# Splitting one zero fill by hand over the sixteen transfer engines

## The chip, the cores and the metric

The kernel runs on one core of a Trainium2 chip. A core has five instruction engines (TensorE, VectorE, ScalarE, GpSimd and SyncE; PE, DVE, ACT, POOL and SP in the profile) and sixteen transfer engines, which carry out the DMAs that SyncE, ScalarE and GpSimd issue. The metric is the time of one execution on the device in microseconds (us). Before the change it is 600.05 us, the median of three runs (599.26 to 600.44).

## The reference

The reference runs one decode step of a transformer block (one token, a window of 4096 cached keys and values, a gated feed-forward part, layer norms modulated by a condition vector) and then its gradients. It returns the output and the gradient of ten inputs:

```python
    _const = dict(B_x=B_x)
    def _f(*_d):
        return _fwd_reference(**{'A_x': _d[0], 'A_k_cache': _d[1], 'A_v_cache': _d[2], 'A_wq': _d[3], 'A_wo': _d[4], 'B_w_gate': _d[5], 'B_w_up': _d[6], 'B_w_down': _d[7], 'c': _d[8], 'w_mod': _d[9], **_const})
    _out, _vjp = jax.vjp(_f, A_x, A_k_cache, A_v_cache, A_wq, A_wo, B_w_gate, B_w_up, B_w_down, c, w_mod)
    _grads = _vjp(grad_out)
```

What matters here are two of these gradients: those of the key cache and of the value cache, each 4 x 65536 x 128 in bf16. The attention reads only the last 4096 rows of the 65536, so in both gradients 61440 of 65536 rows per head group are zero. Those zeros have to be written: 126 MB, about half of all the bytes that the kernel moves.

## The kernel before

The kernel is one long hand-ordered program (no scheduler moves instructions; each engine runs its own in the order in which they were written). Its stages are: loads and the layer norm, the query projection, the scores and the softmax, two large products for the attention's gradient (L637 and L692), the feed-forward part with its three weight gradients (from about L1000), and a last stage, in which VectorE and ScalarE build the gradients of the output projection (`dwo`, stored by L1135), of the modulation weights (`sec`, stored by L1130, and `s2`, L1182), of the query projection (`dwq_tile`, L1178) and of the window's keys and values (`dK` and `dV`, L1171), and store each as soon as it stands. The last stores of that stage are issued by SyncE (`tail = nc.sync`), the others by GpSimd (three small rows, L251, apart).

The zeros are written beside all this, as 120 fills of one megabyte each. A region is 128 rows (partitions of the view, not of SBUF) of 8 KB. An ordinary fill reads a zeroed tile of 128 partitions with 2 KB each in an 8-bit type and writes it as 32-bit zeros, eight rows for each of the sixteen transfer engines. The list `zleft` holds the fills in the order in which `zero(n)` takes them; the tables `Z_Q` to `Z_END` say how many are taken at each point of the program. The last stage takes four (`Z_END = (1, 2, 1, 0, 0)`): number 116 ahead of the `dwo` stores, 117 and 118 together after the sixth `dwo` store, and 119 after the eighth.

Six of the 120 fills are narrow (`NARROW`). Their first eight rows are left to a separate fill at the start, and the rest is written by fifteen transfer engines rather than sixteen. The code does this by resetting the cursor that says at which transfer engine GpSimd's next DMA begins (`inc_swdge_sem(..., mode="reset_dge_cursor")`), issuing a small DMA of five rows (L162, `NS = SKIP + 1` with `SKIP = 4`), which moves the cursor by five, and then one of 120 rows read from 60 partitions (L165). One engine is so left out. The last narrow fill is number 113, just ahead of the last stage.

GpSimd's DMAs share eight semaphores in turn: each waits, on GpSimd, until the eighth DMA before it has landed, which is when all sixteen transfer engines have done their part of it. Within one transfer engine the parts of GpSimd's DMAs run in the order of their issue.

Of the kernel before, what the change touches and what calls it, by code (L numbers as in the profile page):

```python
# [10 lines left out]
P = 128  # L11
FP32 = mybir.dt.float32
# [46 lines left out]
def kernel(  # L59
# [26 lines left out]
    nc = tc.nc  # L86
# [17 lines left out]
    def vt(shape, name, dt=FP32):  # L104
        return pool.tile(shape, dt, name=name)
# [4 lines left out]
    ZW = 4096  # L110
    zeros = vt([P, ZW // 2], "zeros", FP8)
# [12 lines left out]
    for og in (out_2, out_3):  # L124
        for g in range(G):
            region = og[0, g, 0:SKW, :].rearrange("r d -> (r d)").rearrange("(p x) -> p x", p=P)
# [6 lines left out]
    zleft = []  # L133
    while narrow or wide:
        if narrow and (len(zleft) in NARROW or not wide):
            zleft.append((narrow.pop(0), True))
        else:
            zleft.append((wide.pop(0), False))
    nlen = len(NARROW)
    ncount = list(range(1, nlen + 1))  # L140
    NS = SKIP + 1
# [5 lines left out]
    def dep(later, earlier):  # L147
        tc.add_manual_dep(later.ins, earlier.ins.name,
                          mybir.DependencyInfo(mybir.DependencyClass.Sync, mybir.DependencyReason.DATA),
                          reason="pace")  # L150

    def zero(n, after=None):
        for _ in range(n):
            if len(zleft) <= keep[0]:
                return
            region, narrow_ = zleft.pop(0)
            first = None
            if narrow_:
                nc.gpsimd.inc_swdge_sem([], [], mode="reset_dge_cursor")  # L160
                n = nlen - ncount.pop()
                first = nc.gpsimd.dma_start(  # L162
                    out=rest[0:NS, 0:nlen * 128].rearrange("p (t x) -> p t x", t=2)[:, :, n * 64:(n + 1) * 64],
                    in_=zeros[0:NS, 0:64].rearrange("p (t x) -> p t x", t=1).broadcast_to([NS, 2, 64]))
                ins = nc.gpsimd.dma_start(  # L165
                    out=region[8:P, :].bitcast(FP32).rearrange("(t p) x -> p t x", t=2),
                    in_=zeros[0:60, :].rearrange("p (t x) -> p t x", t=1).broadcast_to([60, 2, ZW // 2]))
            else:
                ins = nc.gpsimd.dma_start(out=region.bitcast(FP32), in_=zeros[:, :])  # L169
            if after is not None:  # L170
                dep(first or ins, after)
# [292 lines left out]
    for j in range(KD):  # L464
        if j in (1, 2, 3):
            kT_unit(8 + 2 * j)
            kT_unit(9 + 2 * j)
        if 0 < j <= NT:
            for g in range(G):
                wqT_unit(j - 1, g, "AVAA"[g])  # L470
        for h in range(HQ):
            mm = nc.tensor.matmul(q_ps[:, h:h + 1], lhsT=wq_t[j][:, h * P:(h + 1) * P],
                                  rhs=h1_bf[:, j:j + 1], start=(j == 0 and h == 0), stop=(j == KD - 1),
                                  skip_group_check=True)
        zero(Z_Q[j], mm)
# [8 lines left out]
    for ch in range(8):  # L484
        ps = new_ps("sc_ps")
        for g in range(G):
            mm = nc.tensor.matmul(ps[32 * g:32 * g + 32, 0:512], lhsT=q_col2[:, HG * g:HG * g + 32],
                                  rhs=k_T[:, g, ch * 512:(ch + 1) * 512], start=True, stop=True,
                                  tile_position=(0, 32 * g))
        nc.scalar.copy(out=P_bf[:, ch * 512:(ch + 1) * 512], in_=ps[:, :])  # L490
        nc.vector.reduce_max(out=mx8[:, ch:ch + 1], in_=ps[:, :], axis=AX.X)
        if ch % 2:
            wqT_unit(KD - 1, ch // 2, "AV"[ch // 2 % 2])
        zero(Z_KC[ch], mm)
# [26 lines left out]
    rsum = vt([P, 1], "rsum")  # L521
    last = nc.vector.reciprocal(out=rsum, in_=ssum)
    zero(Z_SM, last)
    rs_ps = new_ps("rs_ps")[:, 0:P]
    nc.tensor.matmul(rs_ps, lhsT=rsum[:, 0:1].broadcast_to([P, P]), rhs=ident_f[:, :], start=True, stop=True)
# [811 lines left out]
```

## Time and profile before

| | |
|---|---|
| median of three runs | 600.05 us (599.26 to 600.44) |
| the profiled execution | 599.91 us, of which the span from the first to the last instruction is 598.1 |
| busy, of the span | PE 68%, DVE 56%, ACT 44%, POOL 27% |
| DMA | 45026 packets, 246.63 MB, 412 GB/s over the span |
| written to HBM, read from it | 185.60 MB, 60.30 MB |
| GpSimd's DMAs | 94.7% of sixteen engines' span |
| SyncE's DMAs | 13.2% |
| zero fills | 114 ordinary ones of 1024 KB, median 15.7 us from issue to landing; 6 narrow ones of 960 KB, 13.1 us |

A row of stretches in the profile gives the stretch, its length, the busy time of PE, PEld (weight loads), DVE, ACT and POOL with the number of instructions in brackets, the granted clock of TensorE, and for DMA the busy share of the sixteen engines and the GB/s that they moved. A row of the timeline gives start, duration, engine, line, operation, what it writes and reads, how many such instructions, and in square brackets how long the engine sat idle before it and what ended that. A row of the chain gives start, duration and what the time went to; the chain is followed back from the last instruction.

### The profile page before, as it was taken

How to read it: one execution, taken by the hardware profiler on the slowest of the kernel's cores; microseconds unless marked ns; L12 is line 12 of the kernel's file. 1: busy time of each engine (PE TensorE's matmuls, PEld its weight loads, DVE VectorE, ACT ScalarE, POOL GpSimd, SP SyncE). 2: the span in 40 equal slices, each digit the busy share in tenths (PEclk: the TensorE clock that was granted, in tenths of full speed). 3: DMA queues.
4: the chain of work that ended last, by engine and by line, in shares of the span. 5: the costliest groups of instructions: out<-in, count | busy, mean ns of one | idle time of the engine just before them, and what ended most of it. 6: DMA issues, size and time to landing. Idle time of an engine off the chain costs nothing.

```text
span 598.1 us, 11044 instructions
## 1 busy us (share of the span) xinstructions
PE 406.6 (68%) x4586; PEld 275.3 (46%) x4612; DVE 335.3 (56%) x641; ACT 265.0 (44%) x409; POOL 159.1 (27%) x253
## 2 busy tenths in 40 slices
PE   3997688999999989999973426245345196775120
PEld 3995334334344546546652426235234175575120
DVE  3654499999511010160018585687787887768170
ACT  2489514567212014213135265565664845883110
POOL 3113123222222212222222243323424263122100
PEclk9999699999999999999995565565555576855555
DMA  8999999999999999999999999999999999999996
GB/s 347 419 418 421 414 423 417 428 424 425 426 419 425 424 428 422 424 422 423 424 396 415 419 409 417 412 359 416 405 403 414 419 422 411 421 424 425 426 424 283
DMA packets 45026, 246.63 MB, mean 412 GB/s; under 512 B 5085, under 2 KB 5085, under 8 KB 24544
## 3 DMA queue, kind: packets, MB, share of 16 engines
q0 software_dynamic: 37536, 217.60, 94.7%
q1 hardware_dynamic: 7392, 28.32, 13.2%
q8 instruction: 36, 0.59, 0.4%
q14 instruction: 14, 0.11, 0.0%
q10 hardware_dynamic: 48, 0.01, 0.0%
HBM read 60.30 MB, written 185.60 MB: 411 GB/s over the span
## 4 chain that ended last, share of the span: by engine, by line
DMA 37%; PE 32%; DVE 17%; issue 5%; ACT 4%; POOL 1%; DVEq 0%; ACTq 0%; POOLq 0%
DMA out_dram<-arena 15%; DMA arena<-in_B_w_gate_dram 13%; PE b_ps L692 10%; DMA out_dram<-zeros 9%; PE n_ps L637 6%; DVE arena L210 6%; DVE arena L206 5%; DVE arena L193 4%; PE t_ps L599 2%; PE tp_side L837 2%; PE tp_wq L454 2%; PE w_ps L395 2%; PE tp_k L435 1%; PE fg L954 1%; ACT arena L456 1%
## 5 line engine op out<-in xcount | busy, mean ns | idle before, releaser
L692 PE MATMUL b_ps<-arena 128*128 128x512 bf16 x493 | 113.4, 379 | 1.1 <-issue 0.2
L169 POOL DMA_DIRECT2D out_dram<-zeros x114 | 62.5, 550 | 176.9 <-DMA out_dram<-zeros 52.8
L193 DVE TENSOR_TENSOR arena<-arena 128x2048 bf16<-128x2048 bf16 x64 | 76.5, 1223 | 2.3 <-PE n_ps L637 0.3
L692 PEld LDWEIGHTS <-arena 128*128 128x128 bf16 x512 | 48.7, 98 | 55.9 <-issue 2.9
L210 DVE CUSTOM_DVE_ANT_0 arena<-arena,scr 128x1024 bf16<-128x1024 bf16 x56 | 66.2, 1220 | 9.6 <-ACT scr L992 9.6
L637 PE MATMUL n_ps<-arena 128*128 128x512 bf16 x249 | 65.1, 378 | 6.9 <-DVE arena L193 5.0
L838 ACT COPY arena<-tp_side 128x1024 bf16<-128x1024 bf16 x54 | 52.8, 1014 | 32.5 <-PE tp_side L837 32.5
L954 PE MATMUL fg<-h_bf,arena 128*128 128x1 bf16 x448 | 16.1, 166 | 55.0 <-DMA arena<-in_B_w_up_dram 31.4
L837 PE MATMUL tp_side<-ident_bf,arena 128*128 128x128 bf16 x432 | 48.9, 297 | 3.7 <-ACT arena L838 1.9
L837 PEld LDWEIGHTS <-arena 128*128 128x128 bf16 x432 | 42.3, 139 | 6.2 <-issue 6.0
L637 PEld LDWEIGHTS <-arena 128*128 128x128 bf16 x256 | 24.6, 97 | 41.6 <-issue 16.2
L954 PEld LDWEIGHTS <-arena 128*128 128x128 bf16 x448 | 14.1, 105 | 58.1 <-DMA arena<-in_B_w_up_dram 33.4
L1166 ACT ACTIVATE arena<-ps_kv 128x512 bf16<-128x512 f32 x48 | 26.1, 680 | 31.1 <-PE ps_kv L1162 30.8
L241 ACT ACTIVATE arena<-scr,h 128x1024 bf16<-128x1024 bf16 x35 | 38.5, 1143 | 2.7 <-DVE dh2acc L210 2.3
L202 DVE CAST arena<-b_ps 128x512 bf16<-128x512 f32 x6 | 4.2, 692 | 61.6 <-PE b_ps L692 61.6
L210 DVE CUSTOM_DVE_ANT_0 arena<-arena,b1k 128x1024 bf16<-128x1024 bf16 x24 | 28.4, 1222 | 17.9 <-PE fg L972 17.9
L1162 PE MATMUL ps_kv<-junk,arena 8*128 8x128 bf16 x256 | 26.5, 299 | 16.7 <-DVE arena L206 14.8
L869 POOL DMA_DIRECT2D out_dram<-arena x28 | 22.2, 798 | 51.5 <-ACT arena L241 35.4
L601 ACT CAST arena<-t_ps 128x512 bf16<-128x512 f32 x56 | 30.1, 589 | 12.1 <-PE t_ps L599 12.1
L1162 PEld LDWEIGHTS <-arena 8*128 8x128 bf16 x256 | 24.6, 138 | 18.4 <-issue 18.4
L456 ACT COPY arena<-tp_wq 128x1024 bf16<-128x1024 bf16 x23 | 21.7, 1041 | 8.1 <-PE tp_wq L454 8.1
L206 DVE TENSOR_SCALAR arena<-arena,cs_col 128x4096 bf16<-128x4096 bf16 (+1 forms) x16 | 16.1, 1019 | 12.5 <-DMA out_dram<-arena 12.4
(305 smaller groups left out, 639.2 us busy)
## 6 DMA issues: line engine op xcount, KB each, us to landing
out_dram<-zeros POOLq DMA_DIRECT2D x114, 1024.0 KB, 15.7
out_dram<-arena POOLq DMA_DIRECT2D x27, 1024.0 KB, 20.4
out_dram<-arena POOLq DMA_DIRECT2D x30, 512.0 KB, 11.6
out_dram<-arena SPq DMA_DIRECT2D x20, 512.0 KB, 10.1
arena<-in_A_wq_dram POOLq DMA_DIRECT2D x8, 1024.0 KB, 20.4
arena<-in_A_wo_dram POOLq DMA_DIRECT2D x8, 1024.0 KB, 12.3
arena<-in_w_mod_dram POOLq DMA_DIRECT2D x7, 1024.0 KB, 17.9
arena<-in_B_w_down_dram SPq DMA_DIRECT2D x14, 512.0 KB, 9.4
```

The source lines that it names most:

```text
L169: ins = nc.gpsimd.dma_start(out=region.bitcast(FP32), in_=zeros[:, :])
L193: return nc.vector.tensor_tensor(out=out, in0=a, in1=b, op=op)
L206: return nc.vector.tensor_scalar(out=out, in0=a, scalar1=s1, scalar2=None, op0=op0)
L210: return nc.vector.tensor_tensor_reduce(out=out, in0=w, in1=b, scale=1.0, scalar=0.0, op0=ALU.mult, op1=ALU.add, accum_out=acc)
L241: return nc.scalar.activation(out=out, in_=b, func=ACT.Copy, scale=col)
L601: nc.scalar.copy(out=o, in_=ps)
L637: mm = nc.tensor.matmul(nbank[k][:, :], lhsT=k_nat[:, g, t_ * DH:(t_ + 1) * DH], rhs=vp[:, t_ % 2, 4 * k:4 * k + 4, :].rearrange("p h d -> ...
L692: mm = nc.tensor.matmul(bbank[p][k][:, :], lhsT=a4[:, p, h, :], rhs=wo_t[u][:, a, k * 512:(k + 1) * 512], start=(i == 0 and a == 0), stop= ...
L837: nc.tensor.transpose(tp[:, i * P:(i + 1) * P], blk[:, i * P:(i + 1) * P], ident_bf[:, :])
L838: nc.scalar.copy(out=blk if dst is None else dst, in_=tp[:, :])
L954: nc.tensor.matmul(gu[:, col:col + 1], lhsT=ug_v[:, q % 2, j // 4, j % 4, k, f0:f0 + 255:2], rhs=h2_bf[:, j:j + 1], start=(j == 0 and i == ...
L1162: nc.tensor.matmul(ps[:, t4 * DH:(t4 + 1) * DH], lhsT=rows[32 * g:32 * g + HG, t_ * P:(t_ + 1) * P], rhs=hd[32 * g:32 * g + HG, :], start= ...
```

## The change

Fill number 117, the first of the two after the sixth `dwo` store, is marked, and `zero` writes it in three DMAs instead of one, after a reset of the cursor: 8 rows read from two partitions, 96 rows read from eight and 24 rows read from six. By the marks in `PARTS`, (transfer engines, rows for each), that is four rows each for engines 0 and 1, twelve each for 2 to 9 and four each for 10 to 15, where the one DMA had eight for each. The rows, their values and their bytes stay the same.

```diff
@@ -136,6 +136,8 @@
             zleft.append((narrow.pop(0), True))
         else:
             zleft.append((wide.pop(0), False))
+    zleft[117] = (zleft[117][0], None)
+    PARTS = ((2, 4), (8, 12), (6, 4))
     nlen = len(NARROW)
     ncount = list(range(1, nlen + 1))
     NS = SKIP + 1
@@ -165,6 +167,16 @@
                 ins = nc.gpsimd.dma_start(
                     out=region[8:P, :].bitcast(FP32).rearrange("(t p) x -> p t x", t=2),
                     in_=zeros[0:60, :].rearrange("p (t x) -> p t x", t=1).broadcast_to([60, 2, ZW // 2]))
+            elif narrow_ is None:
+                nc.gpsimd.inc_swdge_sem([], [], mode="reset_dge_cursor")
+                a = 0
+                for k, rows in PARTS:
+                    ins = nc.gpsimd.dma_start(
+                        out=region[a:a + k * rows, :].bitcast(FP32).rearrange("(p t) x -> p t x", p=k),
+                        in_=zeros[0:k, :].rearrange("p (t x) -> p t x", t=1).broadcast_to([k, rows, ZW // 2]))
+                    first = first or ins
+                    a += k * rows
+                assert a == P
             else:
                 ins = nc.gpsimd.dma_start(out=region.bitcast(FP32), in_=zeros[:, :])
             if after is not None:
```

## The prediction

> **What bounds the kernel now.** Read first: the page's slices and its chain; then busy time by stage of the last 40 us, the end of the chain in order of time, and GpSimd's issues around the changed fill.
>
> ```profile
> span 598.1 us, 11044 instructions
> ...
> DMA  8999999999999999999999999999999999999996
> GB/s 347 419 418 421 414 423 417 428 424 425 426 419 425 424 428 422 424 422 423 424 396 415 419 409 417 412 359 416 405 403 414 419 422 411 421 424 425 426 424 283
> ...
> DMA 37%; PE 32%; DVE 17%; issue 5%; ACT 4%; POOL 1%; DVEq 0%; ACTq 0%; POOLq 0%
> ```
>
> The transfer engines are busy in every slice but the first and the last. After 515 us nothing else matters: PE's share falls, DMA's stays above 1.00 of sixteen engines (packets overlap a little).
>
> ```profile
> 568.20:580.00 11.80, 3.57 (x32) 3.30 (x31) 10.56 (x15) 2.39 (x4) 0.00 (x0) 0.50 1.01 424
> 580.00:590.00 10.00, 0.00 (x0) 0.00 (x0) 0.00 (x0) 0.00 (x0) 0.00 (x0) 0.50 1.02 425
> 590.00:598.10 8.10, 0.00 (x0) 0.00 (x0) 0.00 (x0) 0.00 (x0) 0.00 (x0) 0.50 0.39 162
> ```
>
> From 580 us no engine computes; only transfers are left. Cut into microseconds, the last stretch shows engines dropping out one after another:
>
> ```profile
> 591.00:592.00 1.00, 0.00 (x0) 0.00 (x0) 0.00 (x0) 0.00 (x0) 0.00 (x0) 0.50 0.94 389
> 592.00:593.00 1.00, 0.00 (x0) 0.00 (x0) 0.00 (x0) 0.00 (x0) 0.00 (x0) 0.50 0.63 258
> 593.00:594.00 1.00, 0.00 (x0) 0.00 (x0) 0.00 (x0) 0.00 (x0) 0.00 (x0) 0.50 0.39 160
> 594.00:595.00 1.00, 0.00 (x0) 0.00 (x0) 0.00 (x0) 0.00 (x0) 0.00 (x0) 0.50 0.18 74
> 595.00:596.00 1.00, 0.00 (x0) 0.00 (x0) 0.00 (x0) 0.00 (x0) 0.00 (x0) 0.50 0.06 25
> ```
>
> Full rate is 425 GB/s, so one engine moves 26.6. At 25 GB/s a single engine is working: the last 1.6 us of transfers belong to one engine. The end of the kernel is therefore the finish of the slowest engine, and the question is only which one it is and whether the change gives it more rows or fewer.
>
> **Which engine is last.** The trace has every packet with start, duration, size and queue, but no engine. A packet starts 3 to 4 ns before its engine's previous one ends, so I strung the packets into sixteen chains, backwards from the end. They finish at 596.33, then 594.76, 594.55, 594.52, 594.39, 593.50, 593.40, 593.36, 593.31, 592.91, 592.18, 592.01, 591.85, 591.81, 591.67 and 591.51 us. Of 79 packets of 8 KB between 531 and 575 us that took 311 to 700 ns instead of 309, 76 lie on the chain of 596.33 (two of the other three come right behind a 16 KB instruction fetch). So the last engine is a slow engine, not an unlucky one.
>
> The last narrow fill (L162 and L165, issued at 478.37 and 478.97) tells which engine that is. By the code its first part takes five rows and moves the cursor by five, its second takes 120 rows, eight each, on the fifteen engines after that: the engine at place 4 after the cursor's reset gets none. The sixteen completions of L162 end with 486.72 and 487.20; those of L165 fifteen times follow 2.25 to 2.30 us later, and once 0.19 us later, at 487.39. So the left-out engine was the latest of all, by 0.48 us. In the next two full fills it needs 2.55 and 2.62 us between completions, the others 2.45: the same slowness, packet by packet, as on the chain that ends last. I take place 4 to be that chain. Between 494 and 528 us chains cross and I can't follow it without a break; the reading stands on the signature at both ends.
>
> **The change, part by part.** Program order is the same on PE, DVE, ACT and SP; only the numbers of GpSimd's DMA semaphores shift by two. On GpSimd one issue becomes a cursor reset and three issues, of 8, 96 and 24 rows from 2, 8 and 6 source partitions. It is the fill issued at 494.47:
>
> ```profile
> 485.85 7.36 POOL L1135 DMA_DIRECT2D out_dram<-arena  x5 [3.51 <-DMA out_dram<-arena]
> 493.73 0.75 POOL L1135 DMA_DIRECT2D out_dram<-arena  x1 [0.52 <-DVE arena L206]
> 494.47 0.56 POOL L169 DMA_DIRECT2D out_dram<-zeros  x1
> 496.62 0.55 POOL L169 DMA_DIRECT2D out_dram<-zeros  x1 [1.59 <-DMA out_dram<-zeros]
> 499.41 0.77 POOL L1135 DMA_DIRECT2D out_dram<-arena  x1 [2.24 <-DVE arena L206]
> 502.01 0.53 POOL L1130 DMA_DIRECT2D out_dram<-arena  x1 [1.83 <-DMA out_dram<-arena]
> ```
>
> *Rows.* Before: eight rows of 8 KB on each engine. A fill packet follows the next after 303.7 ns (eight of them and the completion: 2.45 us). Places 2 to 9 get four more, 4 x 0.3037 = +1.21 us each; the other eight get 1.21 us less. Total bytes are unchanged. Place 4 is in the heavy set: +1.21 us. It never idles from there to its end (its chain has no gap but the overlaps named), so nothing absorbs this. Its slowness on fills, 0.10 to 0.17 us for eight rows, adds 0.05 to 0.09 for four: +0.07.
>
> *Two more transfers.* Each leaves a completion packet on each engine: 2.45 less 8 x 0.3037 is 0.02 us. Two: +0.04. A rule speaks for far more: the Trainium skill, "DMA: Bandwidth & Descriptors", section "Anatomy of one DMA — SWDGE (gpsimd) path", fits a transfer at 2.0 us plus its bytes. Taken in full for two transfers that would be +4.0 us, an estimate from that page; back-to-back fills here show the fixed part hidden, and the sum uses 0.02 us.
>
> *GpSimd's issues.* The reset before L162 stands between issues at 477.63 (0.75 long) and 478.37: no time seen; between 0 and the 0.6 us of an issue. Two more issues of 0.6 fall into waits of 1.59, 2.24 and 1.83 us that GpSimd has anyway. Cost 0. If that cover were gone, 1.2 us would delay issues whose transfers reach the engines some 15 to 20 us later: still 0.
>
> *The window of eight.* Each GpSimd transfer waits for the eighth before it. Three parts take three places, so the issues after them wait for transfers two further on, about 2 x 2.5 = 5 us later each: L1135 of 499.41 goes to about 504.4, L1130 of 502.01 to 507, of 511.93 to about 515.5. Behind the waiting instruction stand only GpSimd's next stores; DVE, ACT and SP wait for landings, not issues. The first engine reaches the L1135 of 499.41 at 514 us and the L1130 of 502.01 at 516.6, with 1.2 us less if it is in the light set: 8 us of slack. From 522 us the issues wait for data again, and the window holds only whole transfers. Cost 0; upper bound 5 us if the queue ran dry, which the slack excludes.
>
> *The tail's own chain.* It ends so:
>
> ```profile
> 544.14 24.02 DMA out_dram<-arena
> 568.16 0.03 issue
> 568.18 5.05 DVE arena L206 x8
> 573.23 0.09 issue
> 573.32 1.13 DVEq L1332
> 574.45 4.31 DVE arena L206 x6
> ```
>
> The 24.02 us transfer lands when the slowest engine has done it, so it and the last stores' issues (last at 579.71) move by about +1.3 too. The fastest engine finishes GpSimd's work at 577 (576 if light) and has SyncE's stores from 569 to 571 on: it doesn't run dry, and the slowest is never short. No second cost.
>
> Sum: 1.21 + 0.07 + 0.04 = +1.32 us. The profiled execution (span 598.1, whole 599.91, that is 0.14 under the median of 600.05) would go to 601.2; the median to 601.4. 0.2% of it, 1.2 us, is about what a measurement of this kernel can tell from no change.
>
> **Rivals.**
>
> A. *Another engine ends last: faster.* If the chain of 596.33 is a light one, it drops 1.21 us to 595.12, and the end is whichever is later, that or the best heavy one: one of 594.76 at +1.21 is 595.97. Gain 0.36 to 1.21: 598.8 to 599.7. It decides if the last engine is outside 2 to 9. For it: the break in my chains at 494 to 528 us. Against: the left-out engine was late and slow, and the last chain has its signature. The skill's page "DMA: Bandwidth & Descriptors", section "Latency and other measured facts", says that engines 7 and 15 are usually the slower ones. Were 15 last here, it would be a light one and the case would be this rival's; the narrow fill's completions name place 4 instead.
>
> B. *The rows don't split as said.* If the 96-row part spreads over all sixteen engines (six rows each), place 4 gets between seven and nine rows: -0.3 to +0.3 us, 599.7 to 600.4. For it: no fill of this shape is in the trace. Against: the narrow fill, 120 rows from 60 partitions, did leave one engine out.
>
> C. *More than the rows: a lag that grows.* Instruction fetches, 16 KB packets in queue 8, take about 1.0 us on one engine and set its next completion back by about 1.4; one is at 497.46, one at 515.88. If the shifted issues bring one more onto the slow engine, it is +1.3 + 1.4: 602.8. Nothing says that they move.
>
> **How the numbers follow.** Forecast 0.70, A 0.13, B 0.08, C 0.09. The forecast's rows alone give 1.21 and the other terms only add, but runs of one kernel differ by 1.2 us (599.26 to 600.44), so 0.53 of its 0.70 is slower by over 0.2% and 0.17 within. With C, slower 0.62; with B, within 0.25; A, counted as faster, 0.13. The range takes in B and half of A below and the lower part of C above: 599.6 to 602.3.
>
> **What would show it.** After the change, the last microsecond of transfers is again one engine at 25 GB/s, ending near 597.6; the rate falls from 389 about 1 us earlier than before for the light engines; the transfer that ends the chain lands at about 569.5; three L174 issues start near 494.5, 496.6 and 499. Wrong, if transfers end before 596.3 or no engine works alone for a microsecond.

## The result and the profile after

The changed kernel takes 601.11 us (median of 19 runs, 599.45 to 602.57), the kernel before on the same chips 599.67 (598.44 to 600.87): a ratio of 1.0022 with a 95% interval of 1.0013 to 1.0032, or +1.3 us (+0.8 to +1.9). The profiled execution took 600.93 us with a span of 599.1.

The page of the changed kernel, the span and the transfer engines' two lines:

```profile
span 599.1 us, 11046 instructions
...
DMA  8999999999999999999999999999999999999996
GB/s 349 418 418 420 415 426 411 426 426 423 428 419 425 422 427 424 421 423 425 422 397 412 420 411 416 411 369 413 404 405 416 420 420 412 405 423 427 426 421 266
DMA packets 45250, 246.63 MB, mean 412 GB/s; under 512 B 5309, under 2 KB 5309, under 8 KB 24768
```

The shape is that of before: transfers fill every slice but the first and the last. The bytes are the same, but there are 224 packets more, all under 512 B; the experiments come back to them.

The last stretch of the changed kernel, by microseconds (columns as before):

```profile
590.00:591.00 1.00, 0.00 (x0) 0.00 (x0) 0.00 (x0) 0.00 (x0) 0.00 (x0) 0.50 0.94 389
591.00:592.00 1.00, 0.00 (x0) 0.00 (x0) 0.00 (x0) 0.00 (x0) 0.00 (x0) 0.50 0.92 385
592.00:593.00 1.00, 0.00 (x0) 0.00 (x0) 0.00 (x0) 0.00 (x0) 0.00 (x0) 0.50 0.64 266
593.00:594.00 1.00, 0.00 (x0) 0.00 (x0) 0.00 (x0) 0.00 (x0) 0.00 (x0) 0.50 0.46 188
594.00:595.00 1.00, 0.00 (x0) 0.00 (x0) 0.00 (x0) 0.00 (x0) 0.00 (x0) 0.50 0.39 160
595.00:596.00 1.00, 0.00 (x0) 0.00 (x0) 0.00 (x0) 0.00 (x0) 0.00 (x0) 0.50 0.19 78
596.00:597.00 1.00, 0.00 (x0) 0.00 (x0) 0.00 (x0) 0.00 (x0) 0.00 (x0) 0.50 0.06 25
597.00:598.00 1.00, 0.00 (x0) 0.00 (x0) 0.00 (x0) 0.00 (x0) 0.00 (x0) 0.50 0.02 8
```

The last whole microsecond again belongs to one engine at 25 GB/s, one microsecond later than before, and the last packet ends at 597.38 us instead of 596.33. The rate is at 389 GB/s one microsecond sooner: the tail is longer at both ends, as it must be when some engines have more to do and others less.

The end of the chain of waits of the changed kernel (start, duration, what):

```profile
545.20 24.02 DMA out_dram<-arena
569.23 0.03 issue
569.25 5.67 DVE arena L218 x8
574.92 0.60 DVEq L1344
575.51 4.31 DVE arena L218 x6
```

The same chain as before, 1.06 us later from its transfer on. And GpSimd's issues around the fill, in order of time:

```profile
493.71 0.75 POOL L1147 DMA_DIRECT2D out_dram<-arena  x1 [0.52 <-DVE arena L218]
494.45 0.62 POOL L174 DMA_DIRECT2D out_dram<-zeros  x1
496.59 0.62 POOL L174 DMA_DIRECT2D out_dram<-zeros  x1 [1.53 <-DMA out_dram<-zeros]
499.03 0.67 POOL L174 DMA_DIRECT2D out_dram<-zeros  x1 [1.82 <-DMA out_dram<-arena]
501.55 0.56 POOL L181 DMA_DIRECT2D out_dram<-zeros  x1 [1.85 <-DMA out_dram<-arena]
504.32 1.27 POOL L1147 DMA_DIRECT2D out_dram<-arena  x1 [2.21 <-DVE dcs L222]
506.87 0.53 POOL L1142 DMA_DIRECT2D out_dram<-arena  x1 [1.28 <-DMA out_dram<-arena]
```

No time is to be seen for the reset between 493.71 + 0.75 and 494.45. The three parts go out at 494.45, 496.59 and 499.03, the second and the third each waiting (1.53 and 1.82 us) for a transfer that the one fill would not have waited for, and the next two stores leave at 504.32 and 506.87.

The packets themselves, strung together by their starts, show the slow engine in the stretch of the two fills. One row of 8 KB per entry, start in us and duration in ns; the bar marks the next fill:

```
before  510.81:322 511.09:354 511.40:384 511.73:365 512.05:388 512.39:379 512.70:384 513.04:361
      | 513.40:336 513.68:374 514.01:384 514.35:369 514.65:388 514.99:361 515.31:349 515.62:359
after   510.56:326 510.84:367 511.16:365 511.48:369 511.80:369 512.11:384 512.45:374 512.78:360
        513.09:385 513.43:365 513.75:355 514.07:381
      | 514.48:322 514.75:356 515.06:384 515.39:380 515.73:355 516.03:366 516.34:361 516.66:374
```

Before the change other engines' rows take 322 ns (the first of a DMA) and 348 (each one after it) here, so one engine stands out with mostly 354 to 388. It had eight rows in the changed fill before and has twelve after. From the first row to the next fill's first row it took 2.59 us before and takes 3.92 after: +1.33 us.

Strings of packets can be exchanged where two engines' packets end within a nanosecond or two, and no slow packet marks the engine after 575 us. So that this engine is the one that ends last is a reading. An estimate from the durations agrees with it. At its first row above, before the change, the engine is the twelfth of sixteen to start the fill, 0.15 us ahead of the latest. From there to the end its slow packets take about 1.5 us more in all than the others' of their size (311 to 420 ns against 309, and 355 to 420 against 348), and the last engine ends 1.57 us behind the next.

### The profile page after: what moved, and what is told of

The parts are those of the page before. It is cut to its first block, busy times and chain, and to the rows that moved or that the text cites. A ratio compares the mean times of both kernels' runs of the same rounds, so it can differ in the third digit from the quotient of the medians.

```text
span 599.1 us, 11046 instructions
## 1 busy us (share of the span) xinstructions
PE 406.3 (68%) x4586; PEld 273.9 (46%) x4612; DVE 335.8 (56%) x641; ACT 264.9 (44%) x409; POOL 161.6 (27%) x255
## 4 chain that ended last, share of the span: by engine, by line
PE 45%; DMA 22%; DVE 19%; issue 5%; ACT 5%; POOL 0%; ACTq 0%; DVEq 0%; POOLq 0%; SPq 0%
PE b_ps L704 18%; DMA out_dram<-arena 14%; DVE arena L222 7%; PE n_ps L649 6%; DVE arena L218 5%; DMA arena<-in_B_w_down_dram 4%; DVE arena L205 4%; DMA arena<-in_B_w_gate_dram 3%; PE t_ps L611 2%; PE tp_side L849 2%; PE fold_ps L888 2%; PE tp_wq L466 2%; PE w_ps L407 2%; PE tp_k L447 1%; PE bc_ps L309 1%
```

## The experiments

Each of the kernels below is the changed kernel with the lines shown, and was timed against the kernel before on the same chip. A second measure comes from the packets of the profiled execution: the bytes that GpSimd's and SyncE's queues have still to move, at 508 us and at 528, compared with the kernel before and divided by the full rate. What grows between the two is what the sixteen engines lost, on average, while the changed fill and its neighbours were transferred; in the change itself it is 0.60 us, and after 528 us nothing more is lost.

**Equal rows in three parts.** The split without the redistribution.

```diff
-    PARTS = ((2, 4), (8, 12), (6, 4))
+    PARTS = ((2, 8), (8, 8), (6, 8))
```

> The same three parts after the same reset, but eight rows for every transfer engine: ((2, 8), (8, 8), (6, 8)). Theory 1, the rows decide (the engine at place 4 ends last, and its rows move the end): as before, plus 0.04 us for two more completion packets: ratio 1.000, last packet near 596.4 us, a single engine at the end for 1.6 us. Theory 2, the split itself costs (reset, two more issues, three of eight places in the window): as the changed kernel, ratio 1.0022 to 1.0024, last packet 597.4 or later. Theory 3, another heavy engine than place 4 ends last: as theory 1 here.

Measured: 600.69 us against 599.53, ratio 1.0019 (1.0008 to 1.0030). The split costs about as much as the change does although each engine has its eight rows: theory 1 alone doesn't hold here. The end in the trace is neither theory's: the last packets end at 596.67 and 596.52 us, in an execution of 600.13 us, 0.56 below this kernel's median.

**The heavy eight moved off place 4.**

```diff
-    PARTS = ((2, 4), (8, 12), (6, 4))
+    PARTS = ((5, 4), (8, 12), (3, 4))
```

> The same uneven pattern moved on by three places: four rows each for places 0 to 4, twelve for 5 to 12, four for 13 to 15: ((5, 4), (8, 12), (3, 4)). Place 4 is light now. Theory 1: place 4 ends 1.21 us earlier, at 595.12; of the others the latest, 594.76, ends at 595.97 if it became heavy: the last packet lies between 595.1 and 596.0, ratio 0.9980 to 0.9994. Theory 2, the split costs whatever the rows: ratio 1.0022 to 1.0024. Theory 3: the last engine is one of places 5 to 9, heavy in both: 1.0022; or one of 2 and 3, light here: as theory 1.

Measured: 600.85 us, 1.0017 (1.0005 to 1.0028). The slow engine has four rows here (509.73 to 510.64 us, then eight from 511.12), and the chain that holds 70 of its slow packets between 531 and 575 us ends eighth, at 594.16. Another ends at 596.68. So place 4 was relieved, and the time is still 1 us above before.

**24 rows for places 4 and 5.**

```diff
-    PARTS = ((2, 4), (8, 12), (6, 4))
+    PARTS = ((4, 4), (2, 24), (2, 4), (8, 7))
```

> Twenty-four rows each for places 4 and 5, four each for 0 to 3, 6 and 7, seven each for 8 to 15: ((4, 4), (2, 24), (2, 4), (8, 7)). Sixteen rows more on place 4. Theory 1: its end moves by 16 x 0.3037 = 4.86 us and the slowness of sixteen fill rows, 0.2 to 0.3: +5.1 us, last packet near 601.4, ratio 1.0085. Theory 2: as the changed kernel, ratio 1.002 to 1.003. Theory 3, place 4 is an engine that ends between 591.5 and 594.8: 4.86 us on top of that is 596.4 to 599.7, so +0 to +3.3 us, ratio 1.000 to 1.0055.

Measured: 605.23 us, 1.0088 (1.0071 to 1.0105), +5.7 us by the medians. The slow engine has 24 rows in one run from 510.27 to 517.8, and the chain with 72 of its slow packets ends last, at 600.72:

```profile
598.00:599.00 1.00, 0.00 (x0) 0.00 (x0) 0.00 (x0) 0.00 (x0) 0.00 (x0) 0.50 0.13 53
599.00:600.00 1.00, 0.00 (x0) 0.00 (x0) 0.00 (x0) 0.00 (x0) 0.00 (x0) 0.50 0.11 45
600.00:601.00 1.00, 0.00 (x0) 0.00 (x0) 0.00 (x0) 0.00 (x0) 0.00 (x0) 0.50 0.04 16
```

Two engines at 25 GB/s each until 599.88 us, and then one: rows do count where the slow engine gets them.

**Places 4 and 5 made light, in four parts.**

```diff
-    PARTS = ((2, 4), (8, 12), (6, 4))
+    PARTS = ((4, 10), (2, 2), (2, 10), (8, 8))
```

> Two rows each for places 4 and 5, ten each for 0 to 3, 6 and 7, eight for 8 to 15: ((4, 10), (2, 2), (2, 10), (8, 8)). Theory 1: place 4 ends 1.82 us earlier, at 594.51; the next, 594.76, keeps its eight rows and is then last: -1.57 us, ratio 0.9974, and a candidate that beats both kernels. Theory 2: ratio 1.002 to 1.003. Theory 3, the last engine is among those with ten rows: +0.6 us, 1.001; among those with eight: 1.000.

Measured: 601.55 us, 1.0031 (1.0018 to 1.0044). The slow engine has its two rows (510.10 and 510.40, the next fill from 510.93), and it doesn't help: what the four parts and the ten rows on six other engines cost is more than place 4 gives back. This run alone doesn't divide the two. Between 508 and 528 us these kernels lost 0.86 (equal), 0.64 (moved), 1.10 (24 rows) and 1.00 us (four parts).

What do the parts lose? Two lines of stretches for the changed kernel, then for the three equal parts:

```profile
508.00:512.00 4.00, 2.75 (x53) 2.27 (x53) 2.14 (x12) 4.00 (x7) 0.53 (x1) 1.00 1.11 393
512.00:516.00 4.00, 3.00 (x32) 0.90 (x31) 3.59 (x8) 3.08 (x7) 2.31 (x2) 1.00 1.09 395
```

```profile
508.00:512.00 4.00, 3.36 (x61) 2.40 (x49) 1.86 (x14) 4.00 (x8) 1.01 (x2) 1.00 1.09 377
512.00:516.00 4.00, 2.54 (x27) 0.85 (x27) 4.00 (x7) 1.98 (x5) 0.76 (x1) 1.00 1.10 382
```

and for the kernel before:

```profile
508.00:512.00 4.00, 3.22 (x58) 2.56 (x58) 1.69 (x11) 4.00 (x7) 0.60 (x2) 1.00 1.09 427
512.00:516.00 4.00, 2.69 (x32) 0.71 (x27) 3.91 (x8) 2.61 (x6) 1.00 (x2) 1.00 1.14 423
```

The busy share stays at or above 1.09 while 423 to 427 GB/s become 377 to 395: the engines don't run dry, their packets take longer. Between 506 and 519 us the kernel before has 7 packets that are long (8 KB over 400 ns or 4 KB over 240), the equal parts 43, up to 682 ns for 8 KB, and the change 32, up to 840. And there are new packets of 4 bytes. Both could go back to the shape of the parts: two, eight and six source partitions, hence as many engines, and the others idle. Four more kernels separate this.

**The reset, and one DMA from sixteen source partitions.**

```diff
-    PARTS = ((2, 4), (8, 12), (6, 4))
+    PARTS = ((16, 8),)
```

> The cursor reset and then one DMA of 128 rows, read from 16 source partitions, eight rows of each: every transfer engine gets eight rows, none stands idle. The first four runs left the split itself as the main cost (three parts with eight rows for every engine: 0.19% slower, with 508 to 516 us of the trace at 377 to 382 GB/s in place of 423 to 427). Theory I (parts that leave transfer engines without rows are what costs): 0, within 0.05% of before, 508 to 516 us at 420 GB/s or more. Theory N (each further DMA costs some 0.55 us): 0. Theory S (rows read again and again from a few source partitions cost): as much as the three equal parts, +1.1 us, about 380 GB/s. Theory R (the reset costs): +1.1 us.

Measured: 599.91 us against 599.85, 1.0005 (0.9989 to 1.0021); lost 0.12 us, 10 long packets. Neither the reset nor reading one partition eight times costs anything that shows.

**Three parts, each on all sixteen engines.**

```diff
-    PARTS = ((2, 4), (8, 12), (6, 4))
+    PARTS = ((16, 3), (16, 3), (16, 2))
```

> The reset and then three DMAs of 48, 48 and 32 rows, each on all sixteen engines (three, three and two rows each). Theory I: 0, no long packets between 508 and 516 us. Theory N: +1.1 us, as with the three equal parts. Theory S: between 0 and +1.1 us, since each partition is read two or three times in one DMA. Theory R: +1.1 us.

Measured: 600.14 us, 1.0007 (0.9994 to 1.0020); lost 0.10 us, 11 long packets. Two more transfers in themselves lose next to nothing, so by the packets theory N falls. The time alone would leave room for its 1.1 us (1.0018); the kernels with three parts and other sources below, at most 1.0014 and 1.0004, don't.

**Three parts, engines idle for one row only.**

```diff
-    PARTS = ((2, 4), (8, 12), (6, 4))
+    PARTS = ((16, 7), (2, 1), (14, 1))
```

> The reset and then three DMAs: seven rows for each of sixteen engines, one row for each of two, one for each of the other fourteen. All engines get eight rows, two of the three parts leave engines without rows, but for one row's time only: 16 packets without rows if there is one for each row that a used engine has, where the three equal parts had 256. Theory I: +0.1 us (16 of 256) if it is those packets, and a packet count of 45026 plus 16 plus 32. Theory N: +1.1 us. Theory S: +1.0 us (seven rows from one partition). Theory R: +1.1 us.

Measured: 599.76 us, 1.0010 (0.9996 to 1.0024); lost 0.22 us, and 45074 packets: exactly one packet of 4 bytes for each row that a used engine has, on each engine that has none.

**The source partitions sixteen apart.**

```diff
-    PARTS = ((2, 4), (8, 12), (6, 4))
+    PARTS = ((2, 8), (8, 8), (6, 8))
...
-                        in_=zeros[0:k, :].rearrange("p (t x) -> p t x", t=1).broadcast_to([k, rows, ZW // 2]))
+                        in_=zeros[0:16 * k:16, :].rearrange("p (t x) -> p t x", t=1).broadcast_to([k, rows, ZW // 2]))
```

> The three equal parts (eight rows for every engine, from 2, 8 and 6 source partitions), but the source partitions lie 16 apart instead of side by side. Theory I: +1.1 us as before, 377 to 382 GB/s from 508 to 516 us. Theory N: +1.1 us. Theory S in the form that neighbouring source partitions hinder one another: near 0, no packets of 8 KB longer than 400 ns. Theory S in the form that one partition is read too often: +1.1 us. Theory R: +1.1 us.

Measured: 599.77 us, 1.0000 (0.9986 to 1.0014); lost 0.28 us, 18 long packets, up to 558 ns. The 4-byte packets are all there, as in the equal parts, and partition 0 is still read by three engines; yet most of the loss is gone. That speaks against theory I, and in theory S for the form in which neighbouring partitions hinder one another, though that form expected no row over 400 ns.

**Equal parts, each with source partitions of its own.**

```diff
-    PARTS = ((2, 4), (8, 12), (6, 4))
+    PARTS = ((2, 8), (8, 8), (6, 8))
...
-                a = 0
+                a = o = 0
                 for k, rows in PARTS:
...
-                        in_=zeros[0:k, :].rearrange("p (t x) -> p t x", t=1).broadcast_to([k, rows, ZW // 2]))
+                        in_=zeros[o:o + k, :].rearrange("p (t x) -> p t x", t=1).broadcast_to([k, rows, ZW // 2]))
                     first = first or ins
                     a += k * rows
+                    o += k
```

> The three equal parts (eight rows for every engine) again, but each part reads source partitions of its own, the first 0 and 1, the second 2 to 9, the third 10 to 15, so that the sixteen engines read sixteen different partitions, where they read partition 0 three at a time before. The packets without rows stay: 45314 packets in all. Theory P (several engines reading the same few source partitions is what costs; the sources 16 apart had brought the loss from 0.85 to 0.33 us): 0, 508 to 516 us at 415 GB/s or more, no 8 KB packets over 500 ns. Theory I (the packets without rows, or the idle engines, cost): +0.6 to +1.1 us and about 380 GB/s as with the three equal parts.

Measured: 599.72 us against 599.50, 0.9991 (0.9978 to 1.0004), where the same parts with shared partitions gave 1.0008 to 1.0030 on another chip. The stretches, and the packets of the page (the profiled execution, 601.82 us, is the longest of the twelve):

```profile
508.00:512.00 4.00, 3.54 (x127) 3.25 (x125) 4.00 (x8) 4.00 (x6) 1.00 (x2) 0.78 1.05 406
512.00:516.00 4.00, 2.90 (x58) 2.52 (x58) 1.71 (x11) 4.00 (x7) 2.31 (x3) 1.00 1.17 422
```

```profile
DMA packets 45314, 246.63 MB, mean 411 GB/s; under 512 B 5373, under 2 KB 5373, under 8 KB 24832
```

The packet count of the equal parts is kept; 8 KB packets over 500 ns are gone, 15 long ones are left, and the loss is 0.23 us, of which the 4-byte packets are some 0.1 (256 of them, about 6 ns apart on their engine, over sixteen engines). The first stretch is below the 415 GB/s that theory P expected. Theory P has the place right and the reason too narrow: the partitions sixteen apart were shared between engines as before and lost no more than this. What the cheap kernels have in common is that the sixteen engines' reads don't all lie in partitions 0 to 7, as they do in the change; that crowding is the greater part of the split's cost. What it is about these eight partitions that makes it slow, no run shows.

**The change, with source partitions of its own.** The lines of the kernel just above, with the rows of the change:

```diff
-    PARTS = ((2, 8), (8, 8), (6, 8))
+    PARTS = ((2, 4), (8, 12), (6, 4))
```

> The change as it is (4, 12 and 4 rows), with source partitions of its own for each part. Theory P with the rows of the prediction (place 4 is the last engine and gets four more): +1.2 us, last packet 1.2 us later than that of the equal rows with own sources. Theory P alone (only the sources cost, the rows are absorbed): 0. Theory I: +1.3 us as measured for the change, 393 GB/s from 508 to 516 us.

Measured: 601.00 us against 599.50, 1.0023 (1.0010 to 1.0036); lost 0.24 us instead of 0.60. With the reading made cheap the rows alone cost what the change costs. The kernel just above differs from this one in its rows only and was timed on the same chip: 601.00 against 599.72 is 1.28 us by the medians (1.9 by the two ratios), where the prediction has 1.21 and 0.07 for the rows and the slowness. The chain with 78 slow packets ends last, at 597.02. The expectation's last packet can't be compared, since that of the equal rows comes from their longest execution (598.28).

**24 rows for places 6 and 7.** Own source partitions again.

```diff
-    PARTS = ((2, 8), (8, 8), (6, 8))
+    PARTS = ((6, 4), (2, 24), (8, 7))
```

> 24 rows for engines 6 and 7, four for 0 to 5, seven for 8 to 15, each part with source partitions of its own; the run with 24 rows for 4 and 5 took 5.70 us more than before. If place 4 is the slow engine that ends last (the prediction's reading): 6 and 7 end between 591.51 and 594.76 us before the change, 16 rows more are 4.86 us, so the end goes to between 596.4 and 599.6, +0.1 to +3.3 us, middle value +1.6. If any engine with 24 rows ends so late: +4.8 to +5.7 us.

Measured: 602.25 us, 1.0031 (1.0012 to 1.0050): +1.9 us by the ratio, +2.75 by the medians, within what place 4's reading gave and far from the 5.7 of the pair 4 and 5. That pair had shared sources, but the 1.10 us that its engines lost on average don't make up the difference. The end of this kernel:

```profile
596.00:597.00 1.00, 0.00 (x0) 0.00 (x0) 0.00 (x0) 0.00 (x0) 0.00 (x0) 0.50 0.13 53
597.00:598.00 1.00, 0.00 (x0) 0.00 (x0) 0.00 (x0) 0.00 (x0) 0.00 (x0) 0.50 0.08 33
598.00:599.00 1.00, 0.00 (x0) 0.00 (x0) 0.00 (x0) 0.00 (x0) 0.00 (x0) 0.50 0.07 29
```

Two engines to 597.35, then one to 599.15, neither of them the slow one: its four rows lie from 509.17 to 510.52 us, and the chain with 60 of its packets ends ninth, at 594.01.

**The reverse of the change.** Nine rows for each place but 4 and 5, one for these, own source partitions; meant to beat both kernels.

```diff
-    PARTS = ((2, 8), (8, 8), (6, 8))
+    PARTS = ((4, 9), (2, 1), (10, 9))
```

> The reverse of the change: nine rows for engines 0 to 3 and 6 to 15, one row for 4 and 5, in three parts with source partitions of their own. If place 4 is the engine that ends last and reading different partitions makes the split cheap: place 4 goes from 596.33 to 596.33 - 7 x 0.3037 + 0.25 = 594.45 us, and the next best from 594.76 to 594.76 + 0.30 + 0.25 = 595.31, so the last packet comes 1.0 us earlier and the time is 0.17% below that of before; the chain with the slow packets is no longer the last. If place 4 is not the last engine: +0.3 to +0.6 us, a row more on the last one and the parts' own packets.

Measured: 600.09 us against 600.04, 0.9997 (0.9983 to 1.0010); the last packet ends at 596.91. No gain, and the packets show that in this execution the slow engine was not relieved:

```
        510.80:326 511.08:455 511.50:388 511.83:402 512.18:398 512.52:379 512.86:365 513.18:355 513.49:372
      | 513.86:325 514.14:372 514.47:388 514.81:379 515.13:359 515.45:371 515.77:388 516.08:382
```

Nine rows, not one, and the other engines' packets show where the parts went. An engine with a row in the second part alone would get nine packets of 4 bytes ahead of that row. Instead the two single rows come right behind nine rows and a completion:

```
nine rows from 508.81, completion 511.51:52, one row 511.56:322, next fill from 511.94
nine rows from 509.10, completion 511.80:52, one row 511.85:322, next fill from 512.23
```

Two engines get no row: the next fill's first rows at 509.43 and 510.44 us come behind 23 packets of 4 bytes, as many as the three parts and the store before them leave on such an engine. That accounts for all 128 rows: fourteen engines with nine, two of these with one more, two with none. So the second part fell on two of the first part's four engines: the cursor stood two places on, not four. The third part then began at place 4, and nine rows are what place 4 should get. The runs with 24, four and two rows put the slow engine at place 4 too, and so does the last narrow fill of this very execution, among whose rows no slow packet shows.

Why nine rows from each of four partitions leave the cursor there, where four rows (the pair 4 and 5) and ten (the four parts) let the next part reach place 4, no run shows. So this kernel doesn't relieve the slow engine, and what a relief with own sources and no heavy pair elsewhere would gain is not measured.

## Why the prediction was right, point by point

**What ends the kernel.** Right: the slowest transfer engine, alone at 25 GB/s; predicted to end near 597.6, measured 597.38, which is 1.05 us later than before where 1.32 were forecast. The transfer that ends the chain was expected to land at about 569.5; it lands at 569.22.

**Which engine it is, and its rows.** Right for the change: the packets show twelve rows in place of eight on the slow engine. The terms for the rows, the slowness and the transfers, +1.32 us together, stand against +1.33 us from its first row to the next fill. Five more kernels agree in the count of its rows (four, 24, two, twelve with own sources, and four), and so does the reverse of the change (nine), with the cursor that its packets show. The two pairs with 24 rows, 5.7 us for one and 1.9 to 2.75 for the other, show that it matters which engine gets them. With own sources the rows alone make 1.28 us by the medians.

**Two more transfers, the reset, GpSimd's issues, the window of eight.** Right in size: three parts on all sixteen engines stay within 1.0020, and three equal parts with own sources within 1.0004. The stores forecast for about 504.4, 507 and 515.5 left at 504.32, 506.87 and 516.16, and the queue didn't run dry. The rule of the Trainium skill that was weighed there (page "DMA: Bandwidth & Descriptors", section "Anatomy of one DMA — SWDGE (gpsimd) path", 2.0 us fixed for a transfer) would have made the two cost 4.0 us, an estimate from that page; the runs with three parts and no shared sources exclude it where transfers queue behind one another. Its other rule, on engines 7 and 15 (section "Latency and other measured facts"), can't be held against these traces, which name no engine.

**What the prediction did not have.** The step that costed the split at its completion packets alone failed. All sixteen engines reading from partitions 0 to 7 lengthens packets: 0.60 us lost by the mean engine in the change, 0.86 with equal parts, and with equal parts it showed in the time (+0.5 to +1.8 us). In the change it fell on other engines: of the slow engine's twelve rows none is longer than 388 ns, and with own sources the time is no lower (1.0023 against 1.0022). So the number came out right although a cost was left out, because that cost missed the one engine that decides. That was luck: nothing in the prediction provided for it, and the slow engine isn't spared elsewhere: with 24 rows for places 6 and 7 its four rows took 406 to 581 ns. The two intervals leave room for about 1 us either way, so a small part of it may still be in the result.

**Rivals.** A (another engine ends last, faster) is excluded by the time, which is longer, and B (rows don't split as said) by the packets. B's seven to nine rows were also wrongly worked out: six rows from the 96-row part and none or four from another make six or ten. C (a lag that grows) would have been 602.8, above the interval, and the end moved by 1.05 us, which leaves no room for its 1.4. Between the two instruction fetches that it names it overlooked a third, at 505.84 us, and the fetches did move: the one of 515.88 came at 517.79.

## What to carry to other kernels

Where transfers fill the whole time, the end is one engine's finish: count rows engine by engine, and look for the engine whose packets are slow before moving any. A fill split over fewer engines than sixteen should spread its reads over the source's partitions; crowded onto eight of them, equal parts cost 1.1 us, nearly as much as the moved rows. And a mean over the engines says little: the lost time counts only on the engine that ends last.

## What the runs showed of the hardware

- An engine without rows in a DMA isn't left alone: it gets one packet of 4 bytes (mostly 9 ns) for each row that a used engine has. By the page's counts, less 32 completions for two more DMAs (48 for three): 192 in the change, 256 in the equal parts, 496 with 24 rows on a pair.
- The first 8 KB row of an ordinary fill on an engine takes 322 ns here, the others 348, and one engine's mostly 350 to 400, in every execution looked at.
- Where GpSimd's next DMA begins after a small one doesn't follow from the number of source partitions alone: after nine rows from each of four partitions it began two places on, after four or ten rows from each its rows reached place 4.
- Reads crowded onto partitions 0 to 7 lengthen not only the fill's packets but also the 4 KB packets of the stores beside it (573 to 626 ns for six of them in the change, up to 1181 in the equal parts and 2415 with 24 rows for places 4 and 5, where 160 are usual). The same reads from partitions 0 to 15, one for each engine, or from partitions sixteen apart, do so far less.
